# Pack attention with two expert layers: float32 on-chip w_in, eight-tile products for unit 0, eight banks for the first attention, 1024-column conversion

## The chip, the cores and the metric

The kernel runs on one core of a Trainium2 chip. Its time is device time in microseconds from the first to the last instruction of one launch, as the median of several runs. The engines are TensorE (PE; its weight loads are PEld), VectorE (DVE), ScalarE (ACT), GpSimd (POOL) and SyncE (SP), which issues most transfers. Each engine works its own list of instructions in order and waits on semaphores.

## The reference, cut to what matters

Attention in two steps through 32 pack rows for each head, then a dense layer with a squared ReLU, then a layer of eight experts of which each token takes one:

```python
p_packed = sm_attn(p, k, v)               # 8 batches x 8 heads, 32 pack rows, 576 keys, 64 wide
out = sm_attn(q, p_packed, p_packed)
x = out.transpose(0, 2, 1, 3).reshape(4608, 512)
h = np.maximum(x @ w_in, 0.0)             # w_in 512 x 2048, float64
x = (h * h @ w_out).astype(np.float32)    # w_out 2048 x 512, float64
logits = x @ w_gate + modality_bias[modality_id]; e_idx = np.argmax(logits, axis=1)
gate_w = softmax(logits)[e_idx]
out[mask_e] = gate_w * (np.maximum(x[mask_e] @ w1[e], 0.0) @ w2[e])   # e = 0 .. 7
```

## The kernel before, in words

Products with float32 accuracy are made of three products of a "high" part (fp32r, one fast pass) and a "low" part (the rest). Instead of x @ w_in the kernel multiplies each batch's packed rows with w_in once, 256 x 512 by 512 x 2048 in blocks ("pack products", `pw`), and lets the second attention's weights (`a2T`) multiply that.

**First stage.** Sixteen quads (a batch and four heads) go through `att1` in four steps: scores `s` (L297), softmax (L308 to L315), transposes `ta`, `tb` (L320, L321), and the product `pq` with the values (L329, L330), which yields the float32 pack rows `pp32`, split into `pphl`. The sequence is software-pipelined over the quads. Beside it `conv_in` turns w_in from float64 bit patterns to float32 in 16 pieces of 512 columns, with four DVE operations each (L203 to L212), split into high and low. From the tenth step on, pack products (`pw_unit`, L361: three fp32r matmuls of 512 columns) start.

**Unit 0.** The dense layer works through 12 units of 384 tokens; in each, 16 blocks f of 128 hidden columns: `ph` (layer 1; L474, or L480 to L483 where a unit spans two batches), its ReLU, square and split, then nine `acc` matmuls (L500). While unit 0 runs, `others` makes the remaining pack products (pairs of batches 1 to 3 go through `pws` into the DRAM buffer `pw_d`), and `conv_out` converts w_out in 16 pieces. PSUM then has three acc, two h and three t banks. When unit 1 begins, w_gate is broadcast into `wgb` (2 MB), whose place the conversions used until then; the gate logits of unit u-1 (`tail`, L521 on DVE) run beside unit u.

**Units 1 to 11** reload pack products from `pw_d` (`load_pw`, `split_pw`). The last unit's tail, its routing and the second set of tables stand ahead of the nine expert groups (L787, L809).

The order on each engine is set by a scheduler that takes the program's order, priorities (`high_priority`) and buffer counts; the tables `PW`, `AHEAD` and the rates of `Paced` only set the program's order.

Of the kernel before, what the change touches and what calls it, by code (L numbers as in the profile page):

```python
# [10 lines left out]
F32 = mybir.dt.float32  # L11
# [15 lines left out]
def tile_pack_attention_moe_moe2(  # L27
# [35 lines left out]
    RING, HEAD = 18, 8  # L63
# [12 lines left out]
    AHEAD = 5  # L76
# [20 lines left out]
    pphl = pw_p.tile([P, PAIRS, 2, HP, 2 * P // 2], F32R, name="pphl")  # L97
# [22 lines left out]
    wbt = const.tile([P, NF, 2, DM], F32R, name="wbt")  # L120
    KW, PTW = 2 * S, HP * 2 * NPK
    stage = const.tile([P, 4, 1024], F32, tag="head", name="stage")
    early = const.tile([P, RING - HEAD, 2 * NPC * P], F32, tag="ring", name="early")
    rows = x2_p.tile([P, 2 * KW], F32, name="rows")
    wgf = wgb.rearrange("p e d -> p (e d)")
    vbuf = early.rearrange("p k x -> p (k x)").rearrange("p (i r d) -> p i r d", i=4, d=D)
    vbuf = [vbuf[:, i] for i in range(4)]
    kbuf = [wgf[:, 2048 : 2048 + KW], rows[:, :KW], rows[:, KW : 2 * KW]]
    kbuf = [t.rearrange("p (g s) -> p g s", g=2) for t in kbuf]
    pn = a_p.tile([P, B, HP, NPK], F32, name="pn", bufs=1)  # L130
    ptb = [a_p.tile([P, HP, 2 * NPK], F32, tag="ptb", name="ptb", bufs=2) for _ in range(2)]
    atbuf = [a_p.tile([P, 5, P], F32, tag="atbuf", name="atbuf", bufs=2) for _ in range(2)]
    abuf = [w_p.tile([P, 1024], F32, tag="raw", name="abuf")[:, :S] for _ in range(2)]
# [84 lines left out]
    w_in32 = w_in64.bitcast(I32).rearrange("r (f t) -> r f t", t=2)
    w_out32 = w_out64.bitcast(I32).rearrange("r (f t) -> r f t", t=2)
    NU = 4 * HP  # L220
    PW = {9 + i: [(0, 2 * i), (0, 2 * i + 1)] for i in range(4)}
    PW |= {13 + i: [(1, 2 * i), (1, 2 * i + 1)] for i in range(6)}
    for i in range(3):
        PW[16 + i].append((2, i))
    A20 = 4
    PRI = 0
    a2T = {}

    def conversions(srcs, raws, scs):
        n = len(raws)  # L230

        def load(i):
            if i < NU:
                nc.sync.dma_start(raws[i % n].bitcast(I32).rearrange("p (f t) -> p f t", t=2), srcs[i])

        for i in range(n):
            load(i)
        for i in range(NU):
            w = wbt[:, i]
            raw = raws[i % n].bitcast(I32).rearrange("p (f t) -> p f t", t=2)  # L240
            convert(scs[i % len(scs)], raw, w[:, 0, :], w[:, 1, :])
            load(i + n)
            yield

    def conv_in():
        extra = held["at"].tile([P, 1536], F32, tag="a2T", name="extra", bufs=2)[:, :1024]
        srcs = []
        for u in range(NU):
            fb, hp = divmod(u, HP)
            srcs.append(w_in32[hp * P : (hp + 1) * P, fb * 512 : (fb + 1) * 512, :])  # L250
        return conversions(srcs, [RAWS[0], extra, stage[:, 0], stage[:, 1]], [SCS[0], stage[:, 2], stage[:, 3]])

    def conv_out():
        return conversions([w_out32[u * P : (u + 1) * P] for u in range(NU)], RAWS, SCS)

    def bank(tag, name):
        if "early" in held:
            return held["early"].tile([P, 512], F32, tag="e", name=name, bufs=4)
        return held["all"].tile([P, 512], F32, tag=tag, name=name, bufs={"acc": 3, "h": 2, "t": 3}[tag])


    praw = {}
# [7 lines left out]
    def load_v(i):  # L270
        if i < len(quads):
            b, qd = quads[i]
            vv = vbuf[i % 4]
            nv = 4 * MAIN * D
            nc.sync.dma_start(
                vv[:, :16].rearrange("p x d -> p (x d)"), v[2 * b + qd, :nv].rearrange("(p x) -> p x", p=P)
            )
            nc.sync.dma_start(
                vv[:LAST, 16:].rearrange("p h d -> p (h d)"), v[2 * b + qd, nv:].rearrange("(p x) -> p x", p=LAST)
            )  # L280

    quads = [(b, qd) for b in range(B) for qd in range(2)]
    def att1(i):
# [22 lines left out]
        mx = a_p.tile([P, 1], F32, tag="mx", name="mx")  # L306
        sm = a_p.tile([P, 1], F32, tag="sm", name="sm")
# [7 lines left out]
        nc.scalar.activation(out=a, in_=a, func=AF.Copy, scale=sm)  # L315
# [8 lines left out]
        yield  # L324
        pq = bank("t", "pq")
        for g in range(2):
            ds, ns = slice(2 * g * D, 2 * (g + 1) * D), slice(2 * g * NPK, 2 * (g + 1) * NPK)
# [3 lines left out]
        load_v(i + 4)  # L331
        gs = slice(2 * qd, 2 * qd + 2)
        for j in range(2):
            nc.vector.tensor_copy(
                pp32[j * D : (j + 1) * D, b, gs, j * NPK : (j + 1) * NPK],
                pq[j * D : (j + 1) * D, :P].rearrange("p (g i n) -> p g i n", g=2, i=2)[:, :, j, :],
            )
        hl = pphl[:, b // 2].rearrange("p x g (b n) -> p x g b n", b=2)
        if b < 2:
            places = [(slice(2 * qd + i, 2 * qd + i + 1), (b + i) % 2) for i in range(2)]  # L340
        else:
            places = [(gs, b % 2)]
        for g, o in places:
            src = pp32[:, b, g, :]
            hi = hl[:, 0, g, o, :]
            nc.scalar.activation(out=hi, in_=src, func=AF.Copy)
            nc.gpsimd.tensor_tensor(out=hl[:, 1, g, o, :], in0=src, in1=hi.bitcast(F32), op=ALU.subtract)
        yield

    made = set()  # L350

    def pw_unit(bp, u, so=None):
        if (bp, u) in made:
            return
        made.add((bp, u))
        fb, hp = divmod(u, HP)
        w = wbt[:, u]
        hl = pphl[:, bp]
        ph = bank("t", "pw")
        for i, (x, y) in enumerate(((0, 1), (0, 0), (1, 0))):  # L360
            nc.tensor.matmul(ph, hl[:, x, hp], w[:, y, :], start=(i == 0), stop=(i == 2))  # L361
        if so is None:
            so = pw_p.tile([P, 512], F32, tag="w5", name="pws", bufs=3)
        if bp % 2:
            nc.vector.tensor_copy(so, ph)
        else:
            nc.scalar.activation(out=so, in_=ph, func=AF.Copy)
        cs = slice(fb * 512, (fb + 1) * 512)
        if bp:
            nc.sync.dma_start(pw_d[bp, hp, :, cs], so)  # L370
        else:
# [696 lines left out]
```

## Time and profile before

| | |
|---|---|
| median of 3 runs | 1283.46 us (1280.68 to 1285.04) |
| the profiled execution | 1291.58 us, its span 1289.7 us |
| PE busy | 1235.6 us (96%) |
| DVE, ACT, POOL busy | 834.3, 633.3, 325.2 us |
| mean granted TensorE clock | 0.969 |
| first `ph` of unit 0; first of unit 1 | 144.76 us; 221.85 us |
| DMA | 145.04 MB, mean 112 GB/s |

The clock column gives the granted share of the full TensorE clock: 1.0 is 2.4 GHz, 0.5 is 1.2 GHz, and a mean between them mixes stretches at the two levels. A matmul's row holds its start and a modelled end; rows overlap, so the step from start to start is what a stream costs.

### The profile page before, as it was taken

To read this page: it belongs to the slowest core of one execution; us is meant where nothing else is said; L and a number is where in the kernel's file an instruction comes from. 1 tells how busy PE (TensorE), PEld (TensorE's weight loads), DVE (VectorE), ACT (ScalarE), POOL (GpSimd) and SP (SyncE) were. 2 spreads that over 40 slices of the span, in tenths; PEclk is the share of its full clock that TensorE was granted. 3 is DMA by queue.
4 is the path that set the end of the run, shared out by engine and by line. 5 is a ranking of instruction groups with operands and counts; after the bars stand their busy time and mean duration, and the time that the engine had idled before them with its cause. 6 is when DMAs were issued, how large, how long until landed. Compare 5 with 4: busy or idle time off the path is not lost.

```text
span 1289.7 us, 18073 instructions
## 1 busy us (share of the span) xinstructions
PE 1235.6 (96%) x6100; PEld 1021.7 (79%) x6100; DVE 834.3 (65%) x2168; ACT 633.3 (49%) x1337; POOL 325.2 (25%) x389
## 2 busy tenths in 40 slices
PE   7898989899999999999999999999999999999995
PEld 5566878688888888888888888878787888888884
DVE  4877676687685985779597497988643454354331
ACT  3556466466546765456754576642332333343230
POOL 3644365332101222013221023101220121122011
PEclk6777999999999999999999999999999999999998
DMA  9875665621111222012220112341542442353210
GB/s 335 281 267 185 185 180 176 180 83 50 59 50 33 67 74 67 9 53 74 64 72 20 43 40 87 99 156 42 181 135 90 170 167 97 131 182 115 97 66 36
DMA packets 74167, 145.04 MB, mean 112 GB/s; under 512 B 6608, under 2 KB 26192, under 8 KB 73936
## 3 DMA queue, kind: packets, MB, share of 16 engines
q1 hardware_dynamic: 68304, 124.62, 29.8%
q0 software_dynamic: 5760, 19.17, 4.6%
q8 instruction: 50, 0.82, 0.3%
q14 instruction: 53, 0.43, 0.1%
HBM read 109.92 MB, written 33.85 MB: 111 GB/s over the span
## 4 chain that ended last, share of the span: by engine, by line
PE 74%; DVE 10%; DMA 6%; issue 4%; ACT 2%; POOL 2%; SPq 0%; POOLq 0%; DVEq 0%; ACTq 0%
PE acc L500 24%; PE o L809 13%; PE h L787 12%; PE ph L474 9%; DMA wraw<-in_moe_w 3%; DVE rows L521 3%; PE pq L329 3%; PE pw L361 2%; PE s L428 2%; PE s L297 1%; PE ph L482 1%; PE ph L483 1%; PE ph L480 1%; PE tr L767 1%; DMA wgb<-in_moe_w_gate 1%
## 5 line engine op out<-in xcount | busy, mean ns | idle before, releaser
L500 PE MATMUL acc<-wbt,ghl 128*128 128x512 f32 x1728 | 446.0, 399 | 2.6 <-ACT ghl L491 2.3
L500 PEld LDWEIGHTS acc<-wbt,ghl 128*128 128x128 f32 x1728 | 319.5, 189 | 64.4 <-ACT ghl L491 4.3
L521 DVE SCALAR_TENSOR_TENSOR rows<-rows,wgb 128x512 f32<-128x512 f32 x288 | 213.8, 742 | 6.8 <-DMA wgb<-in_moe_w_gate 3.4
L787 PE MATMUL h<-xt,wbt 128*128 128x512 f32 x864 | 214.2, 398 | 0.4 <-DVE xt L771 0.4
L787 PEld LDWEIGHTS h<-xt,wbt 128*128 128x128 f32 x864 | 162.2, 189 | 39.6 <-DVE xt L771 0.9
L493 DVE TENSOR_TENSOR ghl<-r,ghl 128x384 fp32r<-128x384 f32 x176 | 107.0, 610 | 78.2 <-ACT ghl L491 76.4
L491 ACT ACTIVATE ghl<-r 128x384 fp32r<-128x384 f32 x192 | 99.9, 521 | 82.7 <-PE acc L500 80.8
L820 POOL DMA_INDIRECT out<-wgb,idx_s x36 | 39.2, 1088 | 341.1 <-DVE wgb L818 251.4
L798 DVE SCALAR_TENSOR_TENSOR ht<-h,ht 128x512 fp32r<-128x512 f32 x72 | 48.8, 687 | 113.3 <-ACT ht L797 112.2
L809 PE MATMUL o<-head,ht 128*128 128x512 f32 x432 | 113.8, 398 | 4.8 <-ACT ht L797 4.5
L809 PE MATMUL o<-ring,ht 128*128 128x512 f32 x432 | 111.5, 394 | 0.0
L797 ACT ACTIVATE ht<-h 128x512 fp32r<-128x512 f32 x72 | 42.0, 592 | 140.2 <-PE h L787 139.9
L490 ACT ACTIVATE r<-r 128x384 f32<-128x384 f32 x192 | 99.7, 523 | 4.1
L809 PEld LDWEIGHTS o<-head,ht 128*128 128x128 f32 x432 | 80.6, 189 | 24.7 <-ACT ht L797 5.8
L809 PEld LDWEIGHTS o<-ring,ht 128*128 128x128 f32 x432 | 80.5, 188 | 17.0
L489 ACT ACTIVATE r<-ph 128x384 f32<-128x384 f32 x128 | 61.9, 486 | 63.2 <-PE ph L474 34.7
L405 POOL TENSOR_TENSOR ring<-praw,ring 128x256 fp32r<-128x256 f32 x62 | 51.1, 825 | 156.3 <-ACT ring L404 138.4
L474 PE MATMUL ph<-a2T,ring 128*128 128x384 f32 x420 | 85.6, 339 | 0.0
L474 PEld LDWEIGHTS ph<-a2T,ring 128*128 128x128 f32 x420 | 74.7, 188 | 4.8
L724 DVE TENSOR_TENSOR wbt<-wraw,wbt 128x1024 fp32r<-128x1024 f32 x36 | 44.0, 1223 | 51.0 <-ACT wbt L723 50.5
L474 PE MATMUL ph<-a2T,head 128*128 128x384 f32 x348 | 72.5, 340 | 0.0
L448 POOL TENSOR_TENSOR e<-e,sm 128x256 f32<-128x256 f32 x36 | 28.7, 797 | 171.1 <-DVE sm L447 164.6
(225 smaller groups left out, 1860.3 us busy)
## 6 DMA issues: line engine op xcount, KB each, us to landing
wraw<-in_moe_w SPq DMA_DIRECT2D x72, 512.0 KB, 3.6
praw<-pw_d SPq DMA_DIRECT2D x56, 256.0 KB, 3.8
pw_d<-pws SPq DMA_DIRECT2D x48, 256.0 KB, 3.2
x_d<-rows SPq DMA_DIRECT2D x12, 792.0 KB, 4.2
qT<-in_q SPq DMA_DIRECT2D x36, 256.0 KB, 3.0
early<-in_v SPq DMA_DIRECT2D x16, 512.0 KB, 5.5
rows<-in_k SPq DMA_DIRECT2D x10, 576.0 KB, 7.0
wgb<-in_moe_w_out SPq DMA_DIRECT2D x11, 512.0 KB, 4.1
```

Of the source, the lines that this page charges most:

```text
L405: nc.gpsimd.tensor_tensor(out=t[:, 1], in0=raw, in1=t[:, 0].bitcast(F32), op=ALU.subtract)
L474: nc.tensor.matmul(ph, t[:, x, c, :], a[:, y, c, :], start=(i == 0), stop=(i == 3 * NPC - 1))
L489: nc.scalar.activation(out=r, in_=ph if len(ps) == 1 else r, func=AF.Relu)
L490: nc.scalar.activation(out=r, in_=r, func=AF.Square)
L491: nc.scalar.activation(out=hl[:, 0], in_=r, func=AF.Copy)
L493: eng.tensor_tensor(out=hl[:, 1], in0=r, in1=hl[:, 0].bitcast(F32), op=ALU.subtract)
L500: nc.tensor.matmul(acc[t], hl[:, x, t * P : (t + 1) * P], wbt[:, f, y, :], start=(f == 0 and x == 0 and y == 0), stop=(f == NF - 1 and x = ...
L521: nc.vector.scalar_tensor_tensor(out=junk, in0=row[:, t, :DM], scalar=1.0, in1=wgb[:, e], op0=ALU.mult, op1=ALU.mult, accum_out=one)
L724: nc.vector.tensor_tensor(out=t[:, 1, :], in0=raw, in1=t[:, 0, :].bitcast(F32), op=ALU.subtract)
L787: nc.tensor.matmul(ph, half1[:, g % 2, c, x, f * P : (f + 1) * P], xs[c][:, y, :], start=(i == 0), stop=(i == 3 * NDC - 1),)
L798: nc.vector.scalar_tensor_tensor(out=h[:, 1, :], in0=ph, scalar=0.0, in1=h[:, 0, :].bitcast(F32), op0=ALU.max, op1=ALU.subtract)
L809: nc.tensor.matmul(po, hs[f][:, x, t * P : (t + 1) * P], second(f)[:, y, :], start=(i == 0), stop=(i == 3 * NFE - 1),)
```

## The change

- w_in stays on chip as float32 (eight tiles `w_in` of 128 x 1024), without a high and low part. Conversions work on 1024 columns: an absolute value on ACT, then four DVE operations (a max, an and/shift, two two-input operations). w_out is converted in 8 pieces and split on ACT and POOL as before.
- A pack product (`products`) is eight float32 matmuls, each 64 rows by 32 columns of the array and 512 columns long, on eight different tiles of the array, into two banks. For unit 0 the result is split straight into the ring of blocks (`pw`); for later batches it is copied by ACT and DVE and stored (`pw_out`, 512 KB each, 27 of them). There are 32 products: one in the first stage, 31 in unit 0.
- The first attention runs alone on eight banks: its softmax scale moves to the copy after the value product, which becomes 20 float32 matmuls on four 32-column tiles (`pv`, L339) and two that transpose (`pq`, L351).
- From unit 0 on, PSUM has three acc, one h, two t banks and one two-bank buffer for products; at unit 1 that buffer becomes two h3 banks. `qT`, `om` and `od` have fewer buffers. The last unit's routing and second tables come after expert group 0.

```diff
-    for i, (x, y) in enumerate(((0, 1), (0, 0), (1, 0))):
-        nc.tensor.matmul(ph, hl[:, x, hp], w[:, y, :], start=(i == 0), stop=(i == 2))
...
+    def products(b, f, n):
+        ph = banks("pw")
+        for g, j in ((0, 0), (2, 1), (2, 0), (0, 1), (1, 0), (3, 1), (3, 0), (1, 1)):
+            c = g // 2
+            o = (j + c) % 2 * NPK
+            r = (2 * (g % 2)) * NPK + o
+            nc.tensor.matmul(
+                ph[r : r + NPK, c, : n * P],
+                pp32[j * D : (j + 1) * D, b, g, o : o + NPK],
+                w_in[f // 8 * HP + g][j * D : (j + 1) * D, f % 8 * P : (f % 8 + n) * P],
+                start=True, stop=True, tile_position=(j * D, r),
+            )
+        return ph
+    def pw(b, f, n):
+        ph = products(b, f, n)
...
+            nc.scalar.activation(out=hi, in_=src, func=AF.Copy)
+            nc.vector.tensor_tensor(out=t[:, :, 1], in0=src, in1=hi.bitcast(F32), op=ALU.subtract)
+    def pw_out(i, b, f):
+        ph, so = products(b, f, 4), SO[i % 2]
+        nc.scalar.activation(out=so[:, 0], in_=ph[:, 0], func=AF.Copy)
+        nc.vector.tensor_copy(so[:, 1], ph[:, 1])
+        nc.sync.dma_start(pw_d[b, :, :, f * P : (f + 4) * P], so)
...
+    OUT = [(b, f) for h in (0, 8) for b in range(1, B) for f in (h, h + 4) if (b, f) != (1, 0)]
+    def products0(f):
+        if f in (1, 5, 9):
+            pw(0, f + 3, 4)
+        if f == 12:
+            pw(1, 0, 4)
+        n = len(OUT)
+        for i in range(n * f // NF, n * (f + 1) // NF):
+            pw_out(i, *OUT[i])
...
+            nc.scalar.activation(out=tf, in_=top.bitcast(F32), func=AF.Abs)
+            nc.vector.tensor_scalar(out=tf, in0=tf, scalar1=TOP_MIN, scalar2=None, op0=ALU.max)
+            nc.vector.tensor_scalar(out=t, in0=t, scalar1=0x07FFFFFF, scalar2=3, ...)
+            nc.vector.scalar_tensor_tensor(out=t, in0=top, scalar=-0x40000000, in1=t, ...)
+            nc.vector.scalar_tensor_tensor(out=x, in0=low, scalar=29, in1=t, ...)
...
-        nc.scalar.activation(out=a, in_=a, func=AF.Copy, scale=sm)
...
-            for r in range(4):
-                nc.tensor.matmul(pq[:, ns], vt[:, r, ds], aT[:, r, ns], start=(r == 0), stop=False)
-            nc.tensor.matmul(pq[:, ns], vl[:, ds], aT[:LAST, 4, ns], start=False, stop=True)
+        for r in range(5):
+            k = P if r < 4 else LAST
+            for h in range(4):
+                ns = slice(h * NPK, (h + 1) * NPK)
+                nc.tensor.matmul(
+                    pv[ns, :D], aT[:k, r, ns], (vt[:, r] if r < 4 else vl)[:, h * D : (h + 1) * D],
+                    start=(r == 0), stop=(r == 4), tile_position=(0, h * NPK),
+                )
+        nc.scalar.activation(out=pvs, in_=pv[:, :D], func=AF.Copy, scale=sm)
...
+    held["bufs"] = {"h": 1, "t": 2, "two": 1}
...
-    other = [tail(NUN - 1), route(NTL - UT, NTL)]
-    tables(G_A, G_MAX)
     for g in range(G_ALL):
...
+        if g == 0:
+            pull([route(NTL - UT, NTL)], 100)
+            tables(G_A, G_MAX)
```

On PE, in the middle of unit 0, the pack products (`pw`) stood in threes between the `acc` and `ph` matmuls before:

```order
L500 MATMUL acc<-wbt,ghl 128x512 x7
L474 MATMUL ph<-a2T,head 128x384 x5
L361 MATMUL pw<-wbt,pphl 128x512 x3
L474 MATMUL ph<-a2T,head 128x384 x2
L361 MATMUL pw<-wbt,pphl 128x512 x3
L500 MATMUL acc<-wbt,ghl 128x512 x6
```

Now, between block 7 (whose `acc` stands first here) and the `ph` of block 8, products of eight stand one behind another, with only transposes (`ta`) and scores (`s`) of later tokens between some:

```order
L511 MATMUL acc<-wb_1103,ghl 128x512 x9
L370 MATMUL pw<-wi,pp_82 32x512
L370 MATMUL pw<-wi_113,pp_82 32x512 x2
L370 MATMUL pw<-wi,pp_82 32x512 x2
L370 MATMUL pw<-wi_114,pp_82 32x512 x2
L370 MATMUL pw<-wi,pp_82 32x512
L466 MATMUL ta_1984<-ident,e 128x128 x2
L439 MATMUL s_2091<-pp_82,qT 128x64 x4
```

Four products stand between that `acc` and the `ph` of block 8; the fourth makes that block's weights. Three more stand alone before block 12, and eight behind the last `acc` of unit 0, ahead of the first `ph` of unit 1.

On DVE, unit 1 began like this before; `pws` are copies of pack products, `r` and `ghl` belong to layer 1, and L521 is the gate's first operation, which needs the broadcast w_gate:

```order
L365 COPY pws_1872<-pw 128x512
L459 TENSOR_TENSOR a2T<-ta_1920,a2T 128x2x128
...
L493 TENSOR_TENSOR ghl<-r,ghl 128x384
L446 TENSOR_SCALAR sm<-sm 128x8
L521 SCALAR_TENSOR_TENSOR rows,lg_all<-rows,wgb 128x512
L487 TENSOR_TENSOR r<-ph,r 128x192 x2
```

Now the same place on DVE: six copies of products in a row, then layer 1 of unit 1, then the gate (L532):

```order
L458 RECIPROCAL sm<-sm 128x8
L393 COPY wgb<-pw 128x512 x6
L498 TENSOR_TENSOR r<-ph,r 128x192 x4
L504 TENSOR_TENSOR ghl<-r,ghl 128x384
L498 TENSOR_TENSOR r<-ph,r 128x192
L504 TENSOR_TENSOR ghl<-r,ghl 128x384
L498 TENSOR_TENSOR r<-ph,r 128x192 x2
L532 SCALAR_TENSOR_TENSOR rows,lg_all<-rows,wgb 128x512 x2
```

The copies of products moved to just before unit 1, with the gate three blocks of layer 1 behind them.

## Rows read from the trace of the kernel before

**Rows 1.** Engines by stage: us, busy time of each engine, clock, DMA share, GB/s.

```profile
0.00:145.00 145.00, 124.07 (x635) 89.96 (x636) 95.53 (x225) 73.92 (x150) 66.35 (x97) 0.78 0.76 258
145.00:222.00 77.00, 73.02 (x344) 60.69 (x343) 61.10 (x81) 49.79 (x100) 49.96 (x38) 0.98 0.60 178
222.00:290.00 68.00, 61.65 (x332) 51.42 (x331) 48.79 (x139) 39.40 (x102) 22.92 (x28) 1.00 0.46 136
290.00:858.00 568.00, 563.66 (x2952) 485.78 (x2952) 429.49 (x1375) 339.42 (x785) 110.71 (x136) 1.00 0.20 60
```

**Rows 2.** The same in slices of the first stage.

```profile
0.00:20.00 20.00, 12.14 (x53) 8.49 (x54) 5.11 (x20) 6.46 (x12) 7.58 (x33) 0.79 0.93 317
20.00:40.00 20.00, 16.78 (x79) 11.65 (x78) 15.91 (x33) 10.11 (x22) 11.22 (x15) 0.59 1.05 368
```

**Rows 3.** PE in order of time, 0 to 20 us (start, length, line, operation).

```profile
5.19 2.19 PE L297 MATMUL s<-wgb,ptb 128*64 128x288 f32 x8 [5.19 <-POOL ptb L288]
12.42 1.12 PE L320 MATMUL ta<-ident,abuf 128*128 128x128 f32 x4 [0.26 <-ACT abuf L315]
14.22 1.97 PE L329 MATMUL pq<-atbuf,early 128*128 128x64 f32 x8 [0.47 <-ACT atbuf L322]
16.12 0.69 PE L330 MATMUL pq<-atbuf,early 64*128 64x64 f32 x2
```

**Rows 4.** PE in order of time, 85 to 97 us.

```profile
86.94 1.00 PE L329 MATMUL pq<-atbuf,early 128*128 128x64 f32 x8
87.87 0.43 PE L330 MATMUL pq<-atbuf,early 64*128 64x64 f32 x2
89.17 0.61 PE L320 MATMUL ta<-ident,abuf 128*128 128x128 f32 x4
90.18 1.19 PE L297 MATMUL s<-wgb,ptb 128*64 128x288 f32 x8
```

**Rows 5.** The same, only what runs at 90.1 to 90.35 us.

```profile
90.18 0.46 PE L297 MATMUL s<-wgb,ptb 128*64 128x288 f32 x2
```

**Rows 6.** Where unit 0 and unit 1 begin, PE in order of time.

```profile
144.76 1.55 PE L474 MATMUL ph<-a2T,head 128*128 128x384 f32 x8
...
219.06 0.86 PE L361 MATMUL pw<-wbt,pphl 128*128 128x512 f32 x3
219.76 0.86 PE L500 MATMUL acc<-wbt,ghl 128*128 128x512 f32 x3
...
221.85 0.34 PE L480 MATMUL ph<-a2T,head 128*128 128x384 f32 x1
```

**Rows 7.** Groups on PE, 145 to 235 us (busy us, mean ns).

```profile
L361 PE MATMUL pw<-wbt,pphl 128*128 128x512 f32 x117 | 33.8, 401 | 4.0 <-DVE pws L365 3.3 <-ACT pws L367 0.6
L428 PE MATMUL s<-pp,qT 128*128 128x64 f32 (+1 forms) x40 | 4.0, 252 | 0.0
```

**Rows 8.** Groups on DVE, 145 to 235 us.

```profile
L365 DVE COPY pws<-pw 128x512 f32<-128x512 f32 x20 | 13.4, 680 | 4.4 <-PE pw L361 4.1 <-issue 0.3
...
L209 DVE SCALAR_TENSOR_TENSOR wgb<-wgb 128x512 int32<-128x512 int32 x9 | 9.4, 1044 | 0.1
L206 DVE SCALAR_TENSOR_TENSOR wgb<-wgb 128x512 int32<-128x512 int32 x9 | 8.0, 886 | 0.2
L203 DVE TENSOR_SCALAR wgb<-wgb 128x512 int32<-128x512 int32 x9 | 7.4, 817 | 10.8 <-POOL wbt L216 10.8
...
L206 DVE SCALAR_TENSOR_TENSOR rows<-rows 128x512 int32<-128x512 int32 x4 | 2.8, 690 | 0.1
...
L439 DVE TENSOR_TENSOR e<-s,mx 128x256 f32<-128x256 f32 x4 | 1.7, 421 | 0.2
```

**Rows 9.** DMA issues: number, KB each, us to landing.

```profile
pw_d<-pws SPq DMA_DIRECT2D x48, 256.0 KB, 3.2
...
wgb<-in_moe_w_gate SPq DMA_DIRECT2D x1, 2048.0 KB, 13.0
```

**Rows 10.** DVE in order of time, 232 to 250 us.

```profile
246.26 0.69 DVE L521 SCALAR_TENSOR_TENSOR rows<-rows,wgb 128x512 f32<-128x512 f32 x1 [3.39 <-DMA wgb<-in_moe_w_gate]
```

More of the change, by code (lines that the diff above doesn't have):

```diff
@@ L128, in tile_pack_attention_moe_moe2 @@
[L128 to L133, printed above, removed]
+    KW, VW, SW, AW, PTW = 2 * S, 20 * D, S, 5 * P, HP * 4 * NPK
@@ new lines, in tile_pack_attention_moe_moe2 @@
+    ring = const.tile([P, MOST, 2, NPC, P], F32R, name="ring")
+    QW = HALF // 2
+    wb = [const.tile([P, QW, 2, DM], F32R, tag="wb0", name="wb0")]
+    ec = const.tile([P, QW * 2 * DM], F32, tag="wb1", name="ec")
+    eb = const.tile([P, HALF * 2 * DM], F32, tag="wb2", name="eb")
+    pn = const.tile([P, B, HP, NPK], F32, tag="rtail", name="pn")
+    rows = x2_p.tile([P, UT * XR + DM], F32, name="rows")
+    wgf = wgb.rearrange("p e d -> p (e d)")
+    RAWS = [wgf[:, i * 2048 : (i + 1) * 2048].bitcast(I32) for i in range(2)]
@@ L134, in tile_pack_attention_moe_moe2 @@
+    pvb = sv[9:11]
+    tbuf = [ec[:, 2048:3072]]
+    sv = carve(rows, [AW] * 2)
+    atbuf = [t.rearrange("p (r n) -> p r n", r=5) for t in sv[:2]]
+    w_in = [w_p.tile([P, 1024], F32, tag="raw", name="wi") for _ in range(2)]
+    w_in += [wi_p.tile([P, 1024], F32, name=f"wi{u}") for u in range(2, 2 * HP)]
     for t in ptb:
@@ L245, in conv_in @@
[L245 to L254, printed above, removed]
@@ L256, in bank, with w_out @@
-    def bank(tag, name):
[L257 to L262, printed above, removed]
+    CV = [("i", u) for u in range(4)] + [("o", 0), ("i", 4), ("i", 5), ("o", 1), ("i", 6), ("i", 7)]
+    CV += [("o", u) for u in range(2, NF // 2)]
+    a2T = {}
+    w_in32 = w_in64.bitcast(I32)
+    w_out32 = w_out64.bitcast(I32)
+    def w_out(f):
+        return (wb[f // QW] if f < HALF else wb[2])[:, f % QW if f < HALF else f - HALF]
@@ L324, in att1 @@
         yield
[L325 to L333 removed]
+        pv = bank("t", "pv")
@@ L380, in block @@
[L380 to L399 removed]
+                pp32[j * D : (j + 1) * D, b, gs, o : o + NPK],
@@ new lines, in tile_pack_attention_moe_moe2 @@
+    bg = []
+    runs = []
+    for i in range(len(quads) + 4):
+        if i < len(quads):
+            runs.append(att1(i))
+        for r in (runs if i < 4 else runs[:1] + runs[:0:-1]):
+            next(r)
+        if i >= 4:
+            runs.pop(0)
+        if i % 2 and 3 <= i < len(quads) + 3:
+            pull(cv)
+        if i == 1:
+            pull(cv)
+        if i == 6:
+            bg = [att2(0)]
+        pull(bg)
+        if i == len(quads):
+            pw(0, 0, 4)
+    pull(bg, 100)
```

378 lines of the change are left out of this document (172 added, 206 removed).

## The prediction

> **What bounds the kernel now.** I read the engines by stage first [rows 1]. From 290 to 858 us PE is busy for 563.7 of 568 us at full clock, DVE for 429: units 2 to 11 run at PE's speed, and only less PE work makes them shorter. What the change rewrites lies before that: the first stage to about 145 us, where PE is busy for 124 us at a mean clock of 0.78 and DVE for 95.5, and unit 0 to 222 us, where PE is busy for 73.0 of 77 us. The slices [rows 2] show two things: the clock falls to 0.59 in a slice in which PE is busy for 16.8 of 20 us, and DMA moves 317 to 368 GB/s early on. PE's list in order of time gives a quad's cost at either level of the clock: near 1.2 GHz [rows 3] scores 2.19, transposes 1.12, two value products of 1.97 + 0.69 each, 8.6 us in all; near 2.4 GHz [rows 4] 1.19 + 0.61 + 2 x 1.43 = 4.7 us. Sixteen quads at the mean clock, with 75 pack matmuls, fill the first stage: PE sets its pace. Where unit 0 ends, pack products and layer matmuls alternate without a gap: three `pw` start at 219.06, three `acc` at 219.76, so a pack product's three matmuls cost 0.70 us [rows 6].
>
> **First stage.** Taken out per quad: the ten matmuls of the value product, 2.9 us at full clock. Put in: 20 matmuls of 64 columns on four 32-column tiles, 40 records. The trace has no four tiles; the nearest row is `s` of the second attention, 40 records of 64 columns in 4.0 us, 0.10 each, one after another [rows 7]. So 4.0 us if nothing overlaps, 1.0 if four run at once. The scores speak for overlap: their records take turns on two 64-column tiles, and two of them are done in 0.46 us [rows 5], eight in 1.19 [rows 4], so each further pair costs 0.243 us. I take 1.0. With `pq` (0.4, as the two of L330) and about 1 us in which PE waits for the copy between `pv` and `pq` (estimate: an ACT copy and two hand-overs), a quad costs 1.2 + 0.6 + 1.0 + 0.4 + 1.0 = 4.2 us at full clock, 7.1 at half. A mean of 0.78 is 56% full: 5.5 us. Sixteen are 88 us; with 5.2 us before the first score, 5 us for the second attention of unit 0 and one product, and 4 us until the last quad is through, 102 us. At half clock throughout it would be 16 x 7.1 + 14 = 128. DMA is the other floor: keys and values 18.9 MB, w_in 8.4, two to three pieces of w_out, q and p, together 31 to 32 MB, at 317 to 368 GB/s 84 to 101 us. DVE has its 95.5 us again: fewer operations, but as many elements in three of four passes. I take 111, between 102 and 128 and nearer to 102, since the clock of 0.78 is what the stage shows; ACT's absolute values wait for 1 MB loads in front of later exponentials, so no floor is met exactly. Before it was 144.8: 34 us earlier.
>
> **A product of eight.** 512 columns against 288 of the scores: 0.243 x 512/288 = 0.432 us a record. Two records of a matmul follow each other on one tile. If all eight tiles run at once, 2 x 0.432 + 0.22 (what the first pair of scores took beyond 0.243) = 1.08 us. If the two row halves take turns, 4 x 0.432 + 0.22 = 1.95. If nothing overlaps, 16 x 0.432 = 6.9. I take 1.08: two column tiles overlap in the trace, and the code sends the two halves of each 32-column group to different banks. For the halves no row exists.
>
> The Trainium skill (TensorEngine Tiling (Array Packing), Gotcha 1: PSUM Pressure) says that different row tiles can't write one PSUM bank at the same time. Here each bank gets columns from both halves at once, though never in one group of partitions. By the strict reading a product costs 1.95 us and the 31 of unit 0 27 us more; no row shows it, and the trace's pairs are column tiles only.
>
> **Unit 0.** Before: 16 blocks, 36 packs of 0.70 and three attention sets in 77 us, so (77 - 25.2 - 4)/16 = 3.0 us a block. Now to the end of block 7 and the product that makes the weights of block 8: PE has 8 x 3.0 + 10 x 1.08 + 6 = 41 us. But DVE stands before it in order: six conversions of w_out. With 512 columns the two-input operations took 0.886 and 1.044 us beside POOL, 0.690 without, the one-input 0.817 [rows 8]. Doubled, two of each are 6.0 to 7.1 us; I take 6.3, so 38 us, with eight copies of 0.68 [rows 8], two subtractions of twice that, five score sets of four operations of 0.42 and one of 0.2, 55 us with the three `a2T`; about 1 us more for the first load of w_out, which waits for the last quad: 56, and PE waits.
>
> The rest is 8 x 3.0 + 21 x 1.08 + 4 = 51 us of PE and gaps. There is one product buffer: behind a product PE waits about 1 us (0.68 copy, drain, hand-over) wherever no layer work lies between, twice before block 12. The last five wait for their stores too: 512 KB where 256 took 3.2 us [rows 9], about 3.7, two buffers, so 2.3 us a product, 1.2 each beyond its own. Weights that are split straight into the ring hold PE 3.4 us (block 12 and the first of the end), two score chains behind a single product 4 us. Gaps 15 us: 66. Unit 0 takes 122 us instead of 77. It covers itself no more: eight products stand between its last `acc` and unit 1. Unit 1 begins at 111 + 122 = 233, 11 us later than 221.85 [rows 6].
>
> **What comes back, and the rest.** PE has by then done six attention sets more (1.0 + 0.35 us each) and has not the three packs left over (2.1): 10.2 us that the PE-bound units no longer have. In unit 1 the broadcast of w_gate, 13.0 us [rows 9], now waits for the last store, about 4 us after the last copy; DVE meets the gate after three blocks, some 12 us in, so `ghl` of the next block is late by 6 to 8 us. Before, DVE waited 3.39 us [rows 10] and PE lost 6.4 us in all from 222 to 290 us [rows 1]. I charge 1.5 us. Fewer t banks and buffers in the later units, and the last routing behind expert group 0, I put at nothing: PE there is busy 99% and DVE has a quarter of the time free [rows 1]; 3 us if that cover fails. Sum: 11.2 - 10.2 + 1.5 = +2.5 us on the profiled execution's 1291.58 us. That lies 8.1 above the median, so the median goes from 1283.46 to **1286**: no change that counts, since 0.3% (3.9 us) is about what this kernel's measurement can tell.
>
> **Rivals.**
> 1. *The first stage's gain is kept.* DMA alone sets the first stage (101), and DVE meets less of POOL (its packs' subtractions are gone), so that unit 0 is 91 us of PE work and 13 of gaps: 205, -17 - 10 + 1.5 = -25.5, **1258**. For it: all engines' work before unit 1 falls. Against it: one product buffer and in-order lists.
> 2. *Row halves take turns.* 31 x 0.87 = 27 us on forecast: **1313**. Decided by one number, the length of a product: 1.1 or 1.95.
> 3. *DVE becomes the bound.* Conversions at 7.1 us beside POOL in both stages: the first stage has 16 quads of 1.9, ten conversions and three sets, 109 us busy and not under 122 long; unit 0 gets 126. Unit 1 at 248: **1301**. It decides as soon as DVE is over 90% busy in the first stage.
> 4. *No overlap at all,* the change not doing what it says: 31 x 5.8 = 180 us, **1466**. The pairs of [rows 5] speak against it.
>
> **How the numbers follow.** Forecast 0.43, with its own range 1276 to 1298 (first stage 105 to 120, unit 0 115 to 128); rivals 0.31, 0.11, 0.13, 0.02. Faster by over 0.3%: a fifth of the forecast and nearly all of rival 1, 0.38. Within: 0.18. Slower: nearly half of the forecast, rivals 2 to 4, 0.44. The range, 1254 to 1312, leaves out the fast end of rival 1 and the slow end of rivals 2 to 4, a tenth each.
>
> **What will show it.** First `ph` of unit 0 near 111 us; first two-part `ph` of unit 1 near 233; a product's eight matmuls spanning about 1.1 us from first to last start of the next work; PE idle ahead of the `ph` of block 8 with a DVE subtraction as releaser, and ahead of unit 1's first `ph`; DVE waiting for w_gate. Wrong if `ph` of unit 0 comes after 125 or before 100, if a product takes over 1.5 us, or if units 2 to 11 change by more than the 10 us.

## The result, and the profile after

The changed kernel takes **1300.05 us** (median of 4 runs, 1293.23 to 1301.58) where the kernel before takes 1282.64 (4 runs, 1280.68 to 1285.04): 1.0125 times as long, with a 95% interval of 1.0084 to 1.0165. It is slower by 17.4 us. One later execution of the kernel before fell into a slower state (1354.38 us at a mean clock of 0.84) and stands in no comparison below. The forecast was 1286 and no change that counts; the time lies in its range (1254 to 1312), 2 us above the own range of the likeliest case.

The profiled execution takes 1301.09 us with a span of 1299.3, against 1291.58 and 1289.7 before. So the profiled pair shows 9.5 us of the 17.4; the rest comes last in the point by point section.

First the stages of the kernel after, cut where its first layer product of unit 0, of its block 8, of unit 1 and the first `acc` of unit 2 stand (bounds, length, busy time of PE, weight load, DVE, ACT and POOL with instructions, granted clock, DMA share, GB/s), the answer to [rows 1]:

```profile
0.00:106.00 106.00, 70.75 (x959) 42.95 (x959) 73.80 (x176) 43.16 (x86) 29.57 (x56) 0.77 0.85 304
106.00:173.00 67.00, 54.24 (x338) 35.16 (x339) 45.52 (x62) 34.17 (x60) 29.62 (x25) 0.78 0.46 160
173.00:256.00 83.00, 65.65 (x489) 31.22 (x488) 22.89 (x42) 28.83 (x54) 9.91 (x11) 0.77 0.37 137
256.00:318.00 62.00, 61.67 (x312) 54.14 (x313) 42.58 (x116) 46.80 (x116) 16.86 (x21) 0.95 0.28 94
318.00:869.00 551.00, 547.43 (x2870) 469.23 (x2869) 421.30 (x1359) 326.94 (x751) 102.92 (x128) 1.00 0.19 61
```

The first stage is 39 us shorter (106 instead of 144.8), unit 0 is 73 us longer (150 instead of 77), at a mean clock of 0.77 instead of 0.98, and with PE idle for 30 of 150 us. From unit 2 on nothing has changed: the first `acc` of each unit lies 9 to 12 us later than before, and the last `acc` of all starts at 869.1 us instead of 858.1.

Three rows of PE's list in order of time (start, length, line, operation, then in brackets the idle time before and what ended it) show a product of eight at either level of the clock, and what stands between two of them:

```profile
140.16 1.09 PE L370 MATMUL pw<-wi,pp 64*32 64x512 f32 x16
...
169.38 1.96 PE L370 MATMUL pw<-wi,pp 64*32 64x512 f32 x16
...
199.00 1.09 PE L370 MATMUL pw<-wi,pp 64*32 64x512 f32 x16 [1.53 <-DVE wgb L393]
```

The sixteen records of a product take 1.09 us at 2.4 GHz and 1.96 at 1.2. All eight tiles run at once: cut 0.14 us behind its start, the list holds eight of the sixteen records already.

```profile
140.16 0.66 PE L370 MATMUL pw<-wi,pp 64*32 64x512 f32 x8
```

A record of 512 columns takes 0.43 us at full clock (forecast from the scores), and 1.09 us has room for two rounds of eight, not for four of four. The Trainium skill (TensorEngine Tiling (Array Packing), Gotcha 1: PSUM Pressure) lets no two row tiles at one bank at the same time; here both halves write both banks at once, in other partitions of each, and the measured 1.09 us decides against its strict reading, by which a product would have taken 1.95.

The end of unit 0, all engines in order of time, one period of five:

```profile
247.40 0.60 ACT L392 ACTIVATE wgb<-pw 128x512 f32<-128x512 f32 x1 [2.90 <-PE pw L370]
248.03 0.69 DVE L393 COPY wgb<-pw 128x512 f32<-128x512 f32 x1 [2.80 <-ACT wgb L392]
248.77 0.23 PEld L370 LDWEIGHTS pw<-wi,pp 64*32 64x32 f32 x16 [3.26 <-DVE wgb L393]
248.77 1.96 PE L370 MATMUL pw<-wi,pp 64*32 64x512 f32 x16 [1.53 <-DVE wgb L393]
250.88 0.60 ACT L392 ACTIVATE wgb<-pw 128x512 f32<-128x512 f32 x1 [2.89 <-PE pw L370]
```

A period is 3.49 us: 1.96 of product at half clock, then the ScalarE copy (0.60), then the VectorE copy (0.69), one after the other, and 0.24 of hand-overs. The copies read different banks, and yet the second waits for the first: the program gives it a wait on ScalarE, since both read one tile and write one. What PE waits for in unit 0 (us in total, times, longest):

```profile
PE pw L370 <- DVE wgb L393: 16.3, 11, 3.8
PE ta L466 <- POOL e L459: 6.8, 5, 2.7
PE ph L491 <- DVE wgb L393: 1.5, 1, 1.5
```

Last, unit 0 cut where the clock changes (columns as above):

```profile
106.00:115.00 9.00, 9.00 (x39) 6.65 (x40) 2.73 (x6) 4.05 (x8) 1.01 (x1) 0.50 0.38 140
115.00:149.00 34.00, 29.64 (x205) 20.35 (x203) 25.68 (x30) 21.65 (x40) 20.16 (x16) 1.00 0.41 152
149.00:177.00 28.00, 19.59 (x117) 9.84 (x117) 18.18 (x29) 9.06 (x16) 8.45 (x8) 0.57 0.48 153
177.00:200.00 23.00, 19.68 (x167) 10.86 (x166) 4.50 (x7) 9.64 (x18) 4.03 (x4) 1.00 0.36 138
200.00:208.00 8.00, 6.57 (x48) 2.50 (x41) 1.92 (x2) 3.35 (x6) 0.11 (x1) 0.57 0.27 105
208.00:228.00 20.00, 18.24 (x136) 11.95 (x134) 7.44 (x16) 10.23 (x21) 4.54 (x5) 0.99 0.42 145
228.00:256.00 28.00, 17.16 (x125) 4.24 (x126) 7.97 (x17) 5.01 (x9) 1.23 (x2) 0.50 0.44 158
```

A clock of 0.57 means half clock for 86% of the stretch. PE's busy time at 1.2 GHz is then 9.00 + 0.86 x 19.59 + 0.86 x 6.57 + 17.16 = 48.7 us, work that would take about 24.3 us at 2.4 GHz (estimate: half of it). So a third of the 73 us by which unit 0 grew is neither new work nor waiting, but the clock. Not all of that begins in unit 0: the clock fell at 98.0 us, in the first stage, and PE is busy without a break in the 9 us to 115.

### The profile page after: what moved, and what is told of

The parts are those of the page before. It is cut to its first block, busy times and chain, and to the rows that moved or that the text cites. A ratio compares the mean times of both kernels' runs of the same rounds, so it can differ in the third digit from the quotient of the medians.

```text
span 1299.3 us, 19092 instructions
## 1 busy us (share of the span) xinstructions
PE 1214.8 (93%) x6804; PEld 965.8 (74%) x6804; DVE 806.5 (62%) x2105; ACT 610.9 (47%) x1266; POOL 262.3 (20%) x333
## 3 DMA queue, kind: packets, MB, share of 16 engines
q1 hardware_dynamic: 65456, 123.56, 27.9%
## 4 chain that ended last, share of the span: by engine, by line
PE 70%; DVE 6%; DMA 2%; issue 1%; ACT 1%; POOL 0%; SPq 0%; POOLq 0%; ACTq 0%; DVEq 0%
PE acc L511 23%; PE h L801 15%; PE o L823 15%; PE ph L485 9%; DVE rows L532 3%; PE s L439 1%; DMA wraw<-in_moe_w 1%; PE tr L781 1%; PE ph L493 1%; PE ph L494 1%; PE ph L491 1%; DVE r L498 1%; PE pw L370 1%; DVE ghl L504 1%; DMA wgb<-in_moe_w_gate 1%
## 5 line engine op out<-in xcount | busy, mean ns | idle before, releaser
L511 PE MATMUL acc<-wb,ghl 128*128 128x512 f32 x1728 | 443.3, 400 | 2.7 <-ACT ghl L502 2.6
L511 PEld LDWEIGHTS acc<-wb,ghl 128*128 128x128 f32 x1728 | 320.1, 189 | 68.4 <-ACT ghl L502 6.0
L823 PE MATMUL o<-ring,ht 128*128 128x512 f32 x864 | 219.6, 398 | 2.0 <-ACT ht L811 1.5
L532 DVE SCALAR_TENSOR_TENSOR rows<-rows,wgb 128x512 f32<-128x512 f32 x288 | 214.5, 745 | 4.0 <-DMA wgb<-in_moe_w_gate 0.2
L801 PE MATMUL h<-xt,wb 128*128 128x512 f32 x864 | 214.0, 397 | 0.0
L801 PEld LDWEIGHTS h<-xt,wb 128*128 128x128 f32 x864 | 162.7, 189 | 39.2 <-DVE ht L812 0.4
L823 PEld LDWEIGHTS o<-ring,ht 128*128 128x128 f32 x864 | 160.2, 188 | 40.5 <-ACT ht L811 2.8
L485 PE MATMUL ph<-a2T,ring 128*128 128x384 f32 x696 | 147.1, 348 | 3.0 <-ACT r L500 1.2
L485 PEld LDWEIGHTS ph<-a2T,ring 128*128 128x128 f32 x696 | 124.4, 193 | 20.7 <-issue 7.5
L738 DVE TENSOR_TENSOR wb<-wraw,wb 128x1024 fp32r<-128x1024 f32 x36 | 44.1, 1225 | 50.4 <-ACT wb L737 49.4
L370 PE MATMUL pw<-wi,pp 64*32 64x512 f32 x512 | 46.8, 796 | 17.8 <-DVE wgb L393 16.3
## 6 DMA issues: line engine op xcount, KB each, us to landing
eb<-in_k SPq DMA_DIRECT2D x11, 576.0 KB, 10.6
```

Source lines behind the costliest of these rows:

```text
L370: nc.tensor.matmul(ph[r : r + NPK, c, : n * P], pp32[j * D : (j + 1) * D, b, g, o : o + NPK], w_in[f // 8 * HP + g][j * D : (j + 1) * D, f ...
L485: nc.tensor.matmul(ph, t[:, x, c, :], a[:, y, c, :], start=(i == 0), stop=(i == 3 * NPC - 1))
L511: nc.tensor.matmul(acc[t], hl[:, x, t * P : (t + 1) * P], w_out(f)[:, y, :], start=(f == 0 and x == 0 and y == 0), stop=(f == NF - 1 and x ...
L532: nc.vector.scalar_tensor_tensor(out=junk, in0=row[:, t, :DM], scalar=1.0, in1=wgb[:, e], op0=ALU.mult, op1=ALU.mult, accum_out=one)
L801: nc.tensor.matmul(ph, half1(g % 2, c)[:, x, f * P : (f + 1) * P], xs[c][:, y, :], start=(i == 0), stop=(i == 3 * NDC - 1),)
L823: nc.tensor.matmul(po, hs[f][:, x, t * P : (t + 1) * P], second(f)[:, y, :], start=(i == 0), stop=(i == 3 * NFE - 1),)
```

## The experiments

Each experiment was timed beside the kernel before, whose median was 1281 to 1282.4 us each time. The markers, read from the traces (us):

| kernel | first `ph` of unit 0 | first `ph` of unit 1 | first `acc` of unit 2 | median | ratio to before (95%) |
|---|---|---|---|---|---|
| before | 144.8 | 221.9 | 305.7 | 1282.6 | |
| after | 105.9 | 255.8 | 317.7 | 1300.05 | 1.0125 (1.0084 to 1.0165) |
| copies side by side | 107.7 | 246.9 | 308.4 | 1290.5 | 1.0069 (1.0047 to 1.0092) |
| fillers | 103.0 | 251.7 | 318.2 | 1301.3 | 1.0167 (1.0123 to 1.0212) |
| both | 101.2 | 241.1 | 306.1 | 1294.5 | 1.0098 (1.0064 to 1.0133) |
| 25 products left out | 107.0 | 186.2 | 252.6 | 1236.1 (one run) | |
| late products | 107.7 | 200.7 | 321.2 | 1307.2 | 1.0180 (1.0144 to 1.0217) |
| late, side by side | 107.5 | 195.0 | 308.0 | 1294.8 | 1.0093 (1.0069 to 1.0117) |
| late, side by side, banks | 100.2 | 187.9 | 279.5 | 1271.25 | 0.9915 (0.9895 to 0.9936) |
| late, banks | 102.8 | 186.2 | 280.8 | 1269.6 | 0.9909 (0.9874 to 0.9944) |
| side by side, banks | 100.6 | 236.5 | 300.9 | 1291.4 | 1.0084 (1.0056 to 1.0112) |
| 4 MB less | 100.5 | 247.0 | 308.6 | 1291.7 (one run) | |

Three theories of why unit 0 grew stood at the start. A: the copies in series cost the time. B: the clock does. C: VectorE's list in order, with six conversions in it, is the bound of blocks 0 to 7.

**Copies side by side.** The two copies are declared independent, so that each waits for PE alone:

```
-        nc.scalar.activation(out=so[:, 0], in_=ph[:, 0], func=AF.Copy)
-        nc.vector.tensor_copy(so[:, 1], ph[:, 1])
+        c0 = nc.scalar.activation(out=so[:, 0], in_=ph[:, 0], func=AF.Copy)
+        tc.add_to_no_dep_group(f"po{i}", c0.ins)
+        c1 = nc.vector.tensor_copy(so[:, 1], ph[:, 1])
+        tc.declare_no_dep(c1.ins, group=f"po{i}", reason="two banks, two readers")
```

> The two copies behind a stored product (ACT one bank, VectorE the other) no longer wait for one another. Theory A (copies in series): the gap behind a product with nothing after it falls from 1.53 us to about 0.9, eleven waits on the VectorE copy lose 0.6 to 0.7 us each, the first gate-free block of unit 1 (first two-part ph, 255.75 us in the changed kernel) comes 7 to 12 us earlier, if the clock is as it was. Theory B (the clock alone sets the length of unit 0): at 1.2 GHz a product still costs 1.96 us, and the gap shrinks by 0.6 us only in the eight products of the end: 5 us earlier at most. Theory C (VectorE's list in order is the bound): no change beyond 2 us.

1290.54 us, 9.5 below the changed kernel by the medians, 10.6 by the spans (1288.7 against 1299.3), and some 7 by the ratios to the kernel before (1.0069 against 1.0125). The end of unit 0 in this kernel:

```profile
240.30 0.69 DVE L394 COPY wgb<-pw 128x512 f32<-128x512 f32 x1 [2.20 <-PE pw L370]
240.35 0.60 ACT L392 ACTIVATE wgb<-pw 128x512 f32<-128x512 f32 x1 [2.30 <-PE pw L370]
241.14 1.96 PE L370 MATMUL pw<-wi,pp 64*32 64x512 f32 x16 [0.94 <-DVE wgb L394]
```

The gap is 0.94 us instead of 1.53, a period 2.9 instead of 3.49, and the product still runs at half clock. Unit 0 takes 139.2 us instead of 149.9. A holds at the size that it named; it leaves 62 of the 73 us.

**Fillers.** One matmul into a bank that nobody reads stands behind each of the last eleven products:

```
+        if i >= 16:
+            idle = bank("t", "idle")
...
+                nc.tensor.matmul(idle[:, :512], ident, SO[(i - 1) % 2][:, 0, :512], start=True, stop=True)
```

With both edits together the filler has 384 columns.

> Behind each of the last eleven stored products one more matmul of 512 float32 columns into a bank that nobody reads, its moving operand the copy of the product before. Copies stay in series. Theory B (the clock falls because PE stands still in the gaps): these products run at 2.4 GHz, 1.09 us instead of 1.96, and the gaps of 1.53 us hold the 0.87 us of the extra matmul: unit 1 begins 6 to 9 us earlier. Theory A alone (copies in series, clock a by-product that the filler cannot hold): products stay at 1.96 us, the extra matmul takes 1.7 us in a gap of 1.53, and unit 1 begins 1 to 3 us later.

> Both edits: copies side by side and an extra matmul of 384 float32 columns behind each of the last eleven stored products. If A and B both hold and add up: a product of the end costs 1.09 us and 0.9 us of gap, 2.0 instead of 3.5, so 12 us earlier in the last eight and 5 to 8 us in the other waits: unit 1 begins 12 to 20 us earlier, and the whole is as fast as the kernel before or up to 6 us faster. If the clock cannot be held: 5 to 8 us earlier.

With fillers alone 1301.26 us: nothing gained, and unit 1 begins 4.1 us earlier, between what the two theories said. The clock did rise; at the end of unit 0 the products run at full clock:

```profile
241.33 1.12 PE L397 MATMUL idle<-wgb,ident 128*128 128x512 f32 x2 [0.81 <-ACT wgb L392]
242.38 1.09 PE L370 MATMUL pw<-wi,pp 64*32 64x512 f32 x16
```

From the first `ph` of block 8 to unit 1 (164 to 252 us) the granted clock is 0.89, where it was 0.77. But the filler does not lie in the gap: it starts only when the ScalarE copy is through (0.81 us of standing still), and then holds PE for 1.05 us from its start to the next product's. A period is 2.95 us instead of 3.49. The filler's bank is one of the two that the second attention uses, and more of that attention runs in unit 1 (24 records of scores and 6 of transposes behind its first `acc`, where the changed kernel has 8 and none), so that the first `acc` of unit 2 comes no earlier; that the bank is the reason is not shown. With both edits 1294.47, no better than side by side alone. So B's cause is right (less standing still, higher clock) and filling is no remedy: what the clock gives back, the eleven fillers take, 1.05 us each. (PE is busy for 26.4 us of unit 0 at half clock instead of 49.4, worth about 11.5 us; 7.5 of its 31 products run there instead of 14.) With both edits unit 1 did begin 14.6 us earlier, as expected, but the whole missed its band, which ended at the time of the kernel before.

**25 products left out.** Here `pw_out` makes only its first two products and stores them again and again.

> Leaves out 25 of the 27 stored products with their copies (the same two results are stored again and again, so the later batches are computed from wrong weights). Theory B with A: the 25 products cost unit 0 their PE time of 1.1 to 2.0 us, the waits behind them and a part of the half clock, 55 to 65 us of 150: unit 1 begins near 190 to 197. Theory C (conversions of w_out on VectorE are the bound of blocks 0 to 7): the ph of block 8 stays within 5 us of 173 us, and unit 1 begins no earlier than 205.

Unit 1 begins at 186.2 us, earlier than any theory said, and block 8 of unit 0 at 143.1 instead of 173.0. The two stretches (107 us to block 8, and on to unit 1):

```profile
107.00:143.00 36.00, 34.81 (x226) 24.53 (x226) 19.67 (x27) 22.33 (x40) 15.15 (x13) 0.95 0.88 309
143.00:186.00 43.00, 35.41 (x172) 28.05 (x172) 24.79 (x38) 23.46 (x45) 23.67 (x20) 0.88 0.68 250
```

C falls by its second number: all six conversions of w_out are through when unit 1 begins, with VectorE busy for 44.5 of 79 us, where C had 205 or later. Its first number, block 8 within 5 us of 173, is missed too, but this run can't judge it. VectorE's order moved with the edit: up to 143 us only two conversions are through here (L251 is the last of a conversion's four operations) and a third has begun, while the changed kernel does all six before its block 8.

```profile
L251 DVE SCALAR_TENSOR_TENSOR wgb<-wgb,tb 128x1024 int32<-128x1024 int32 x1 | 1.4, 1428 | 0.0
...
L251 DVE SCALAR_TENSOR_TENSOR rows<-rows,tb 128x1024 int32<-128x1024 int32 x1 | 1.3, 1264 | 0.0
```

There VectorE is busy for 45.5 of the 67 us before block 8. Its work does not fill them, but the lists in order do hold PE up: the longest wait of PE in unit 0 ends with a copy of a product that stood behind the split of a conversion on ScalarE (L257) and a score chain on VectorE (L457):

```profile
161.33 1.21 ACT L257 ACTIVATE wb<-wgb 128x512 fp32r<-128x512 f32 x2 [2.95 <-DVE wgb L251]
...
162.75 0.57 ACT L392 ACTIVATE wgb<-pw 128x512 f32<-128x512 f32 x1
...
163.33 1.29 DVE L457 TENSOR_SCALAR sm<-sm 128x8 f32<-128x8 f32 x1
164.54 0.68 DVE L393 COPY wgb<-pw 128x512 f32<-128x512 f32 x1
...
165.28 1.96 PE L370 MATMUL pw<-wi,pp 64*32 64x512 f32 x16 [3.83 <-DVE wgb L393]
```

The last `acc` comes 65.3 us earlier (803.8 against 869.1): a stored product cost 65.3/25 = **2.6 us** (a single run) where its matmuls take 1.09 at full clock. PE's busy time at half clock in unit 0 falls from 49.4 to 11.3 us.

**Late products.** If the price is the place, another place is cheaper. Twelve products that are loaded again only from unit 2 on go behind the first twelve blocks of unit 1:

```
+    LATER = [x for x in OUT if x[0] > 1 and x[1] >= 8]
+    OUT = [x for x in OUT if x not in LATER]
...
-            if u == 1:
+            if u == 2:
                 st1.close()
...
-            ph = bank("h3" if u else "h", "ph")
+            ph = bank("h3" if u > 1 else "h", "ph")
...
+                if u == 1 and f < len(LATER):
+                    pw_out(100 + f, *LATER[f], SO=[w_in[i] ... for i in (2, 3)])
```

> Twelve of the 27 stored products (columns 1024 to 2047 for batches 2 to 7) are made in unit 1, one behind each of its first twelve blocks; w_in and the product banks stay until unit 2, and unit 1 uses the one layer bank of unit 0. Copies in series as in the changed kernel. Theory (a product costs 2.6 us in unit 0, where 25 of them were worth 65 us, because PE waits behind it and half of them run at 1.2 GHz; in unit 1 PE has layer work to go on with, at 2.4 GHz, 1.1 us each): 12 x 1.5 = 18 us off, first acc of unit 2 at 298 to 302 us instead of 317.7, and the whole at 1280 to 1284. Rival (the one layer bank holds PE up in unit 1, or a product's price is the same wherever it stands): 0 to 6 us off, 1294 to 1300.

> The same, with the two copies of a stored product side by side. If both savings add: the 15 stored products left in unit 0 lose 0.6 us in about half of the cases, 4 to 6 us more than with copies in series: first acc of unit 2 at 293 to 297 us, the whole at 1275 to 1279, which is faster than the kernel before. If the late products take away the places in which parallel copies helped (the eight at the end of unit 0): within 2 us of the other run.

1307.19 and 1294.84 us: no gain. The theory is missed; the first run lies even above its rival's band, and the second, 12 us below the first, is in neither of its bands. Unit 1 begins 52 to 55 us earlier, and all of it is lost within unit 1. With copies side by side it takes 104.9 us from its first `acc` to that of unit 2. Its layer products, in order of time:

```profile
265.31 0.36 PE L496 MATMUL ph<-a2T,ring 128*128 128x384 f32 x1
266.48 0.44 PE L493 MATMUL ph<-a2T,ring 128*128 128x384 f32 x1 [0.81 <-DVE r L500]
266.76 0.36 PE L495 MATMUL ph<-a2T,ring 128*128 128x192 f32 x2
266.96 0.36 PE L496 MATMUL ph<-a2T,ring 128*128 128x384 f32 x1
268.20 0.45 PE L493 MATMUL ph<-a2T,ring 128*128 128x384 f32 x1 [0.89 <-DVE r L500]
```

Behind each part of a block PE waits for the passes of ScalarE and VectorE that empty the one layer bank (8.0 us in these waits, of 19.8 in which PE stands idle in unit 1; 9.7 more end in front of products, with ScalarE), and the clock is at half for 17.1 us. The product banks, which now live until unit 2, took the two banks that unit 1 had.

**Banks dealt out anew.** In units 0 and 1 the layer products get two banks and the second attention one:

```
-    held["bufs"] = {"h": 1, "t": 2, "two": 1}
+    held["bufs"] = {"h": 2, "t": 1, "two": 1}
...
-            tp = bank("h3" if g else "t", "tr")
+            tp = bank("h3" if g else "h", "tr")
```

(and `pc` and `pl` of the routing from "t" to "h"). With late products and copies side by side:

> The kernel with late products and copies side by side, with the banks dealt out anew in units 0 and 1: two for the layer products, one for the second attention's scores and transposes (the routing's small products and the first group's transposes use the layer banks). Theory (late products cost 1.1 us each, and the one layer bank of unit 1 ate their gain: there PE waited for the VectorE and ScalarE passes over one bank between the parts of a block, some 36 us): unit 1, from its first acc to that of unit 2, takes 68 to 74 us instead of 104.8, the first acc of unit 2 comes at 272 to 280 us instead of 308, and the whole takes 1252 to 1265. Rival (the 12 late products hold up unit 1 by their copies on ScalarE and VectorE, whatever the banks): unit 1 still takes 90 to 105 us, the whole 1285 to 1295.

The same banks with all products in unit 0:

> The same dealing of the banks with copies side by side, but all 27 stored products in unit 0. Theory (the products' place is what costs): the layer work of unit 0 waited for its bank 1.2 us and the scores chain gets one bank less: within 4 us of the kernel with parallel copies alone (1290.5), and unit 0 as long as there (139 us) within 5 us. Rival (the banks, not the place of the products, are what gains): 1262 to 1275 here too.

With late products **1271.25 us**, faster than both kernels (0.9915 of the kernel before, 0.9895 to 0.9936); with all products in unit 0 1291.41. So the banks alone gain nothing, and late products without them nothing; together they are worth about 20 us. The first `acc` of unit 2 comes at 279.5 us, in the expected band, but only because unit 0 began at 100.2 us instead of 107.5, which the theory did not name: unit 1 takes 81.7 us where 68 to 74 were expected, and the whole is 6 us above its band. In the stages of this kernel (unit 0 to block 8, the rest of unit 0, unit 1 between the two first `acc`) the clock is near full throughout, and PE stands idle for 5.6 us in unit 1 instead of 19.8:

```profile
100.00:144.00 44.00, 37.41 (x242) 26.13 (x242) 28.17 (x33) 25.67 (x46) 19.68 (x17) 0.96 0.49 156
144.00:188.00 44.00, 38.34 (x262) 25.02 (x263) 19.23 (x31) 21.66 (x43) 14.98 (x15) 0.92 0.33 118
198.00:280.00 82.00, 76.41 (x533) 51.88 (x533) 53.20 (x141) 49.34 (x121) 17.49 (x22) 1.00 0.56 185
```

and a late product costs its 1.09 us and no gap, since layer work stands on either side:

```profile
245.81 1.80 PE L513 MATMUL acc<-wb,ghl 128*128 128x512 f32 x7
247.54 1.09 PE L370 MATMUL pw<-wi,pp 64*32 64x512 f32 x16
248.56 0.45 PE L493 MATMUL ph<-a2T,ring 128*128 128x384 f32 x1
```

**The same with copies in series.**

> Late products with the banks dealt out anew, but the copies of a stored product in series as in the changed kernel. If parallel copies matter only where nothing stands behind a product: 1271 to 1276, within 4 us of the run with parallel copies (1271.25). If a copy in series delays the layer work's passes on VectorE and ScalarE in unit 1 as well: 1278 to 1285.

1269.6 us: the same within what can be told. With late products and these banks, A is worth nothing that shows in the time.

**4 MB less.**

```
-                nc.sync.dma_start(raw, src)
+                if n < 4 or kind == "o":
+                    nc.sync.dma_start(raw, src)
```

> Leaves out the loads of the second half of w_in (4 MB of the first stage's 32; its conversions run on what an earlier load left, so these weights are wrong). Theory (DMA, full until 80 us, sets the first stage): the transfers end 10 to 12 us earlier and the first ph of unit 0 comes at 94 to 98 us instead of 105.9. Rival (PE with its waits and the clock sets it): ph within 3 us of 105.9, and DMA's share falls below 0.95 before 80 us.

5.4 us earlier (100.5), between the two expectations. In the changed kernel DMA is full from 20 to 80 us; with 4 MB less it is not, and VectorE is:

```profile
40.00:60.00 20.00, 14.84 (x162) 8.97 (x153) 16.91 (x41) 9.10 (x20) 7.14 (x7) 0.67 1.04 371
```

```profile
40.00:60.00 20.00, 13.00 (x174) 7.68 (x166) 19.77 (x40) 7.76 (x16) 4.60 (x4) 0.76 0.78 251
```

The first fence is the changed kernel, the second this one. That DMA bounds the first stage is not shown: this is a single profile, and the stage ended between 100.2 and 107.7 us in the nine other experiments, which left its loads alone. What it shows is that with less DMA VectorE is the one that is full from 40 to 60 us.

## Why the prediction was right or wrong

1. *First stage: 111 us, 34 earlier.* Measured 105.9, 38.9 earlier. The size is right within 5 us. Three floors of 102, 101 and 95.5 us were named; DMA and VectorE are each full in some slice (the run with 4 MB less), and which of the three ends the stage stays open. Rival 3 wanted VectorE over 90% busy here: it was busy for 73.8 of 106 us, 70%.
2. *A product of eight: 1.08 us.* Measured 1.09. Right: the trace of before had only pairs of column tiles, and the price of a record read from them [rows 4, 5] held for eight. Rivals 2 and 4 fall. The number that was to decide rival 2, 1.1 or 1.95, does so only beside the granted clock: at half clock these products take 1.96.
3. *DVE stands before PE in blocks 0 to 7: 56 us.* Measured 67 us to block 8, and mostly for another reason. VectorE was busy for 45.5 us of it, where the step's terms add up to 56.6 (it wrote 55): a conversion takes 1.00 + 1.07 + 1.45 + 1.28 = 4.8 us on VectorE and not 6.3 (mean durations of its four lines in unit 0). PE stood idle for 12.8 us, near the 15 of the forecast; 6.9 of them end with VectorE's copies of products, and the wait ahead of block 8 (1.32 us) with POOL and not with a subtraction on VectorE. But PE itself was busy for 54.2 us instead of 41, 23 of them at half clock (see 5). Rival 3 falls with its condition, though the time, 1300, is the 1301 that it named: by the time alone it would look right.
4. *Gaps of about 1 us, 2.3 us a product at the end, for the stores.* Measured 1.53 and 3.49, of which 0.87 is the half clock. The copies do not run side by side, and the stores do not hold: with copies side by side the gap is 0.94. Yet PE's idle time in unit 0, 30 us of 150, is what the prediction's waits add up to (15 before block 8, 15 in gaps; measured 12.8 and 17.4).
5. *Unit 0: 122 us.* Measured 149.9. **This is the step that failed**: it added up PE's work at full clock. It counted 41 + 51 = 92 us of PE work; PE was busy for 119.9, and 24.3 of these are there only because 48.7 us ran at 1.2 GHz. The work itself was about 95.6 us, and unit 0 at full clock would have taken about 125.6. Rival 1, with 104 us for unit 0, falls too. The first stage was reckoned at its granted clock, unit 0 by rows of a unit that stood at 0.98 before [rows 1]; but there it had 4 us of idle time, and the same prediction put 30 us of waits into it. The Trainium skill (TensorE: Matmul & The Clock Gate, A second HAM failure mode: psum-queue depth-cycling) tells of such a case, with bf16 matmuls: small waits between groups of matmuls that go round PSUM banks let the clock swing between its two levels. The trace agrees: 14 of the 31 products of unit 0 run at half clock, and with fillers 7.5.
6. *What comes back: 10.2 us less 1.5 for w_gate.* Measured from 33.9 us late at unit 1's first `ph` to 11.0 late at the last `acc`: 22.9 come back. The marker misled: in the kernel before, 19.4 us lie between the first `ph` of unit 1 (221.85) and its first `acc` (241.3), with work of unit 0 in between; now 5.7, so 13.7 of the 22.9 are no gain but the place of the marker. And PE, idle for 6.35 us from 222 to 290 us before [rows 1], is idle for 0.33 in 256 to 318 us. Of the 6.35, 3.2 ended with the VectorE pass over `ph` that stands in one list with the gate; VectorE no longer waits for w_gate (0.2 us in all, line 532 on the page of the profile). The stall that the forecast charged with 1.5 us did not come.
7. *Units 2 to 11 unchanged.* Right, 9 to 12 us late throughout; from the last `acc` to the end 430.2 us instead of 431.6.

The sum by its terms, on the profiled pair: +2.5 forecast, -5.1 (step 1), +27.9 (step 5), -14.2 (step 6), -1.4 (step 7): +9.7, measured +9.6. Errors of opposite sign hid most of each other: that the time lies in the range is in part luck.

*The base.* The prediction took the change on the profiled execution over to the median. That execution of the kernel before was a poor one: 1291.58 us at a mean clock of 0.969, while its later runs beside the experiments take 1278 to 1288 us at 0.969 to 0.981. The profiled one of the changed kernel, at 0.948, is like its other runs (0.948 to 0.959). Some 8 of the 17.4 us are that difference, and not in any row of the two profiles.

## What to carry to other kernels

A piece of PE work that waits for its own copies costs its matmuls, the gap, and the half clock of what stands around it: here 2.6 us for 1.09, in one run without them. Put such pieces singly between long runs of other matmuls, and check whose banks they hold there; both together took this change from 1300 to 1270 us (1271 with the copies side by side), neither alone took it below 1290. And set a stage's clock in a forecast by the waits that the forecast itself puts into the stage, not by the stage's clock before.

## What the runs showed of the hardware

- Eight 64x32 tiles, four column groups in two row halves, run at once: 16 records of 512 float32 columns in 1.09 us at 2.4 GHz and 1.96 at 1.2, with both halves writing the same two banks in different partitions.
- In the changed kernel the clock fell to 1.2 GHz at 227.7 us, behind a wait of PE of 1.06 us (for POOL) and within one of 1.21 (for VectorE), stayed there while seven products followed each other with gaps of up to 1.53 us, and was back at 2.4 GHz at 261.9, when the layer products of unit 1 ran without a gap. With fillers behind the products it was at 2.4 GHz from 230.2 to 250.7 us, in the same part of unit 0.
- Of the kernel before, two executions at a mean clock of 0.969 took 1291.58 and 1288.46 us, those at 0.974 to 0.981 took 1278 to 1286; within the second group the clock does not order them.
